# Attention and two feed-forward layers on one core: where the second layer's weights are split and parked

## The chip, the cores and the metric

One core of a Trainium2 chip runs the kernel. Its engines are TensorE (PE in the tables, with PEld for its weight loads), VectorE (DVE), ScalarE (ACT) and GpSimd (POOL); SyncE (SP) issues nearly all DMAs, in order, from one queue. Each engine works through its own list of instructions in order and waits on semaphores. The metric is the device time of one execution in microseconds (us). The kernel before takes 1095.94 us, the median of three runs (1095.74 to 1098.24).

## The reference

`x` is chunked attention over 3072 tokens (8 heads of 64, so 512 columns; each chunk of 32 queries sees 56 keys and 8 memory slots). Two feed-forward layers follow, both 512 to 2048 to 512 columns:

```python
h = x @ w_in                                  # layer 1
x = (h - np.tanh(h)) @ w_out
h = x @ w_in2                                 # layer 2
g = np.maximum(h, 0.0) + alpha * np.minimum(h, 0.0)
out = g @ w_out2
```

The weights come as 64-bit floats. The kernel works in 32 bits and carries each operand as a high part and a low rest, so that a product is three matmuls (high by high, high by rest, rest by high).

## The kernel before, in words

**Layer 1, blocks 0 to 3.** The first 2048 tokens go through attention and layer 1 in four blocks of 512. A block runs over sixteen slices f of 128 hidden columns: 12 matmuls of 128x512 for h (L320), tanh and subtraction (L334, L335), the split of g into `gh` and `gl` (L342, L343), 12 matmuls for y (L361). Attention of the next tokens runs in between: scores into `sp` (L674, in block 0 L716), softmax, values into `pv` (L800). In block 0 all 32 weight words of layer 1 (a word is a 128x512 slice, W_in in tiles `ri`, W_out in `ro`) are loaded and converted from 64 bits, and split into `wt`. Block 0's order is written out by hand; from there on a scheduler places the instructions of each engine.

**The pair and layer 2.** The last 1024 tokens go through layer 1 in another way, and all 3072 tokens through layer 2 in that way too: with seven products of half-size operands in place of eight. There are four such blocks: b = 0 is the pair (layer 1's last 1024 tokens), b = 1 to 3 are layer 2. Each has eight pairs of h slices (`pair_h`, 42 matmuls L455 a pair) and then a y stage (L569). The seven products need sums of weight slices, so the weights are also prepared once in that form and written to DRAM, which the code calls parking: `w1i`, `w1o` for layer 1 and `w2i`, `w2o` for layer 2. The h of block b reads `w1i` or `w2i` by DMA (`wi`, L416), its y `w1o` or `w2o` (`wo`, L407).

**Parking** is a list of steps (`park_plan`). Layer 1's 48 steps take words that are already split. Layer 2's 64 steps load a 64-bit word into `pk` (L105), convert it in two passes on VectorE (L116 `u`, L129 `wv`) and one on ScalarE (L125, from 16 bits to 16 bits, in place), split it (L139, L140), form two or four sums `sm` (L165 to L170 for W_in, L205 to L210 for W_out), split those into `ws`, and store all of it. Four steps make two words into one group: the first word, the second word, the two halves of the sums. W_in and W_out groups alternate. `PARKS` says how many steps go into which block: blocks 0 to 3 and the pair's first four slices. A step's loads are issued ahead of it, its stores right behind it.

**What sets the order.** Raw words and sums live in the pool `w`, which has 35 places; layer 1's weights hold 32 of them until the last block lets them go one by one. In that last block, from f = 2 on, `stage["roomy"]` lets a load go one step earlier. The converted low word `u` lies in the PSUM pool `ps_a`, two banks, which attention's scores `sp` also use. The pair's products 5 and 7 lie in `ps_y` (four banks), in `ps_a` for its first slice.

Of the kernel before, what the change touches and what calls it, by code (L numbers as in the profile page):

```python
# [7 lines left out]
FP32 = mybir.dt.float32  # L8
# [21 lines left out]
PARKS = ((2, 30, 32), (34, 0, 32), (34, 0, 32), (28, 0, 27), (14, 0, 16))  # L30
# [10 lines left out]
def chunk_attention_two_ffn_kernel(  # L41
# [55 lines left out]
    def load_raw(l, i, name):  # L97
# [15 lines left out]
    def shift_word(raw):  # L113
        pool, tag = (ps_y, "y") if stage.get("early") else (ps_a, "a")
        u = pool.tile([128, 512], U32, tag=tag, name="u")
        nc.vector.tensor_scalar(  # L116
            out=u, in0=words_of(raw)[0], scalar1=13, scalar2=None, op0=ALU.logical_shift_right
        )
        return u

    def top_word(raw):
        def part(dtype, k):
            return raw.bitcast(dtype).rearrange("p (n four) -> p n four", four=4)[:, :, k]

        nc.scalar.activation(out=part(FP16, 3), in_=part(BF16, 2), func=ACTF.Copy)  # L125

    def merge_words(raw, u, dst=None):
        s = t_p.tile([128, 512], U32, tag="t", name="s") if dst is None else dst.bitcast(U32)
        nc.vector.scalar_tensor_tensor(  # L129
            out=s, in0=words_of(raw)[1], scalar=0xffff0000, in1=u, op0=ALU.bitwise_and, op1=ALU.bitwise_or  # L130
        )
        return s.bitcast(FP32)

    def to_f32(raw, dst=None):
        top_word(raw)
        return merge_words(raw, shift_word(raw), dst)
# [7 lines left out]
    sw = {}  # L144

    def park_in(f):
        raw = raws.pop((1, 2 * f))
        v = aw.tile([128, 512], FP32, tag="v", name="wv")
# [4 lines left out]
        if odd:  # L153
            split_f32(v[:, 256:512], w[:, 0:256], w[:, 256:512])
            nc.sync.dma_start(out=w2i[p][:, 3072:3584], in_=f32(w)[:, 0:512])
        else:
            split_f32(v, w[:, 0:512], w[:, 512:1024])
            nc.sync.dma_start(out=w2i[p][:, 0:1024], in_=f32(w))

    def park_sum(p, half, to=None):  # L160
# [15 lines left out]
        nc.sync.dma_start(out=(to or w2i)[p][:, c:c + 1024], in_=f32(w))  # L176

    def park_op(m, p, src, to=None):
        c = 512 * (p % 2)
        dst = (to or w2o)[m][p // 2][:, c:c + 512].rearrange("k (a n) -> k a n", a=2)  # L180
        nc.sync.dma_start(out=dst, in_=f32(src))
# [7 lines left out]
    def park_out(f):  # L189
        raw = raws.pop((1, 2 * f + 1))  # L190
        v = aw.tile([128, 512], FP32, tag="v", name="wv")
# [24 lines left out]
    def first_in(p):  # L216
        for odd in range(2):
            w = wts[2 * p + odd, 0]
            v = sw[odd] = aw.tile([128, 512], FP32, tag="v", name="wv")
            add = nc.vector.tensor_tensor if odd else nc.gpsimd.tensor_tensor  # L220
            add(out=v, in0=f32(w[:, 0]), in1=f32(w[:, 1]), op=ALU.add)
            if odd:
                dst = w1i[p][:, 3072:3584].rearrange("p (a n) -> p a n", a=2)
                nc.sync.dma_start(out=dst, in_=f32(w)[:, :, 256:512])
            else:
                nc.sync.dma_start(out=w1i[p][:, 0:1024], in_=f32(w).rearrange("p a n -> p (a n)"))

# [27 lines left out]
    def park_plan():  # L255
        order = [(2 * p + j, side) for p in range(NF // 2) for side in range(2) for j in range(2)]
        loaded = [0]

        def step(fn, *args, n=0):
            def go():  # L260
                n1 = n + (1 if n and stage.get("roomy") else 0)
# [14 lines left out]
        for p in range(NF // 2):  # L276
            for k, (one, total) in enumerate(((park_in, park_sum), (park_out, park_out_sum))):
                n = 4 * p + 2 * k
# [3 lines left out]
                yield step(total, p, 1, n=n + 3)  # L282

# [152 lines left out]
    def split_x2(b, m):  # L436
# [3 lines left out]
        split_f32(f32(src), hi, lo)  # L440
# [33 lines left out]
    def pair_h(i, ahead=None, mid=None):  # L474
# [11 lines left out]
        for m in (1, 6, 5, 7) if p % 2 else (6, 1, 5, 7):  # L486
# [138 lines left out]
    astack = ExitStack()  # L625
# [652 lines left out]
```

## Time and profile before

| what | value |
|---|---|
| time, median of 3 | 1095.94 us |
| profiled execution, its own time | 1097.9 us |
| its span, first to last instruction | 1096.1 us |
| mean granted TensorE clock | 0.982 |
| PE busy | 1045.6 us, 95% of the span |
| DVE, ACT, POOL busy | 768.6, 613.1, 513.0 us |
| DMA | 259.12 MB, mean 236 GB/s |

The stages lie in time like this: attention's start to 28.6 us, block 0 to 137.8, blocks 1, 2 and 3 to about 242.5, 356 and 470.5, the pair's h to about 556, its y to 639, and then layer 2's h and y stages by turns (the first h 639 to 706.5). A stage in which PE is busy to the full gains nothing from other engines' idle time; the time that can be won is where PE is idle or its clock is below full, which is 1.00 in the tables (2.4 GHz; the other level is 1.2 GHz, and a mean between them is a mixture).

### The profile page before, as it was taken

To read this page: it belongs to the slowest core of one execution; us is meant where nothing else is said; L and a number is where in the kernel's file an instruction comes from. 1 tells how busy PE (TensorE), PEld (TensorE's weight loads), DVE (VectorE), ACT (ScalarE), POOL (GpSimd) and SP (SyncE) were. 2 spreads that over 40 slices of the span, in tenths; PEclk is the share of its full clock that TensorE was granted. 3 is DMA by queue.
4 is the path that set the end of the run, shared out by engine and by line. 5 is a ranking of instruction groups with operands and counts; after the bars stand their busy time and mean duration, and the time that the engine had idled before them with its cause. 6 is when DMAs were issued, how large, how long until landed. Compare 5 with 4: busy or idle time off the path is not lost.

```text
span 1096.1 us, 17823 instructions
## 1 busy us (share of the span) xinstructions
PE 1045.6 (95%) x6582; PEld 848.1 (77%) x6582; DVE 768.6 (70%) x1044; ACT 613.1 (56%) x942; POOL 513.0 (47%) x428
## 2 busy tenths in 40 slices
PE   6999999999988799979999999999999999999998
PEld 5777788777766578766778888888788888888886
DVE  6687777778555666668588845689755789656883
ACT  5888654444546676745364446655256844456650
POOL 6576778888655677966221512213322206123100
PEclk8999999999999899989999999999999999999999
DMA  9998545466578888959747867277685289682575
GB/s 327 340 321 277 179 176 212 158 197 219 187 237 264 290 291 296 373 175 410 300 154 247 302 212 249 84 249 235 226 300 199 77 272 306 203 284 87 156 213 168
DMA packets 133095, 259.12 MB, mean 236 GB/s; under 512 B 39056, under 2 KB 73872, under 8 KB 133008
## 3 DMA queue, kind: packets, MB, share of 16 engines
q1 hardware_dynamic: 124368, 251.43, 67.1%
q10 hardware_dynamic: 8640, 6.56, 1.9%
q8 instruction: 52, 0.85, 0.3%
q14 instruction: 35, 0.29, 0.1%
HBM read 184.54 MB, written 73.40 MB: 235 GB/s over the span
## 4 chain that ended last, share of the span: by engine, by line
PE 55%; DVE 3%; DMA 2%; ACT 1%; issue 1%; POOL 0%; SPq 0%; DVEq 0%; ACTq 0%
PE yb L569 27%; PE h L455 25%; PE y L361 1%; PE h L320 1%; DMA wo<-w2o 1%; DMA x<-x0d 1%; DMA pk<-in_moe_w_out_dram 1%; DVE u L116 0%; DMA wi<-w1i 0%; ACT pk L125 0%; DVE wv L129 0%; DVE gb L477 0%; DVE gb L465 0%; DVE xt L431 0%; DVE sm L169 0%
## 5 line engine op out<-in xcount | busy, mean ns | idle before, releaser
L455 PE MATMUL h<-xh,wi 128*128 128x512 f32 x896 | 283.0, 392 | 10.6 <-ACT hv L508 7.1
L569 PE MATMUL yb<-goh,wo 128*128 128x512 f32 x896 | 278.8, 389 | 0.7 <-DMA wo<-w2o 0.7
L455 PEld LDWEIGHTS h<-xh,wi 128*128 128x128 f32 x896 | 169.1, 189 | 50.6 <-ACT hv L508 8.0
L569 PEld LDWEIGHTS yb<-goh,wo 128*128 128x128 f32 x896 | 168.2, 188 | 36.0 <-DMA wo<-w2o 1.1
L320 PE MATMUL h<-ring,wt 128*128 128x512 f32 x768 | 189.3, 395 | 1.1 <-DVE t L335 1.1
L569 PE MATMUL yb<-gol,wo 128*128 128x512 f32 x448 | 174.4, 389 | 0.6 <-DVE gol L542 0.6
L320 PEld LDWEIGHTS h<-ring,wt 128*128 128x128 f32 x768 | 143.8, 189 | 34.5 <-DVE t L335 3.2
L517 POOL TENSOR_TENSOR t<-gb,ga 128x512 f32<-128x512 f32 x32 | 45.2, 1414 | 245.8 <-DVE ga L470 203.7
L361 PE MATMUL y<-gh,wt 128*128 128x512 f32 x512 | 135.9, 405 | 11.3 <-ACT gh L342 8.2
L361 PEld LDWEIGHTS y<-gh,wt 128*128 128x128 f32 x512 | 95.7, 192 | 36.7 <-ACT gh L342 10.2
L455 PE MATMUL h<-xl,wi 128*128 128x512 f32 x256 | 99.9, 390 | 0.0
L569 PEld LDWEIGHTS yb<-gol,wo 128*128 128x128 f32 x448 | 84.1, 188 | 18.4 <-DVE gol L542 1.0
L140 POOL TENSOR_TENSOR ws<-sm,ws 128x512 fp32r<-128x512 f32 x64 | 85.6, 1342 | 20.7 <-ACT ws L139 18.6
L343 POOL TENSOR_TENSOR gl<-t,gh 128x512 fp32r<-128x512 f32 x64 | 87.2, 1363 | 14.6 <-ACT gh L342 7.2
L551 ACT ACTIVATE goh<-ga 128x1024 fp32r<-128x1024 f32 x48 | 48.5, 1051 | 55.2 <-DVE ga L542 47.9
L140 POOL TENSOR_TENSOR x<-x,xh 128x1024 fp32r<-128x1024 f32 x12 | 34.6, 2898 | 94.6 <-ACT xh L139 94.5
L542 DVE TENSOR_TENSOR gol<-ga,goh 128x1024 fp32r<-128x1024 f32 x48 | 65.0, 1381 | 19.0 <-ACT goh L551 19.0
L542 DVE TENSOR_TENSOR gol<-gb,goh 128x1024 fp32r<-128x1024 f32 x48 | 70.2, 1488 | 10.0 <-ACT goh L551 10.0
L551 ACT ACTIVATE goh<-gb 128x1024 fp32r<-128x1024 f32 x48 | 49.6, 1054 | 48.8 <-DVE gb L542 43.9
L455 PE MATMUL h<-x,wi 128*128 128x512 f32 x192 | 75.2, 392 | 0.0
L361 PE MATMUL y<-gl,wt 128*128 128x512 f32 x256 | 70.5, 396 | 0.7 <-POOL gl L343 0.7
L469 ACT ACTIVATE n<-n,alpha_neg 128x512 f32<-128x512 f32 x96 | 64.9, 719 | 0.4
(116 smaller groups left out, 1694.0 us busy)
## 6 DMA issues: line engine op xcount, KB each, us to landing
wo<-w2o SPq DMA_DIRECT2D x84, 512.0 KB, 4.6
wi<-w2i SPq DMA_DIRECT2D x72, 512.0 KB, 5.8
wo<-w1o SPq DMA_DIRECT2D x28, 512.0 KB, 4.5
wi<-w1i SPq DMA_DIRECT2D x24, 512.0 KB, 7.7
kn<-in_k_dram SPq DMA_DIRECT2D x24, 384.0 KB, 5.6
vn<-in_v_dram SPq DMA_DIRECT2D x24, 384.0 KB, 4.2
w1i<-ws SPq DMA_DIRECT2D x16, 512.0 KB, 4.1
w1o<-ws SPq DMA_DIRECT2D x32, 256.0 KB, 2.8
```

What stands on the lines that cost most here:

```text
L140: nc.gpsimd.tensor_tensor(out=lo, in0=v, in1=f32(hi), op=ALU.subtract)
L320: last["ffn"] = nc.tensor.matmul(out=h, lhsT=wi[:, a, kk, :], rhs=ring[c][:, s0:s0 + n, kk, :], start=(i == 0), stop=(i == 3 * KD - 1),).ins
L343: nc.gpsimd.tensor_tensor(out=gl, in0=t, in1=f32(gh), op=ALU.subtract)
L361: mm = nc.tensor.matmul(out=yp[l, b][j][:, :n * 128], lhsT=wo[:, a, j * 128:(j + 1) * 128], rhs=g[c], start=first, stop=final,)
L455: nc.tensor.matmul(out=h, lhsT=w[:, a, 128 * kt:128 * kt + 128], rhs=x[c][:, kt, :], start=(first and j == 0), stop=(j == 5), skip_group_c ...
L469: nc.scalar.activation(out=n, in_=n, func=ACTF.Copy, scale=alpha_neg[:, f:f + 1])
L517: nc.gpsimd.tensor_tensor(out=d3, in0=gb[1], in1=ga[1], op=ALU.subtract)
L542: last["prep"] = nc.vector.tensor_tensor(out=out, in0=p, in1=q, op=op).ins
L551: nc.scalar.activation(out=hi, in_=src, func=ACTF.Copy)
L569: last["yy"] = nc.tensor.matmul(out=yd[b, into][i], lhsT=w[:, a, i], rhs=op[c][:, p % 2], start=(m == into and p == 0 and n == 0), stop=(p ...
```

## The change

- The plan of layer 2's parking first makes all W_in words, then all W_out words. It is thinner in layer 1 (27, 27 and 24 steps in blocks 1 to 3, in place of 34, 34 and 28) and ends earlier in block 3. The W_out words, 32 steps, lie in the pair's h (16 steps over its first six slices) and in layer 2's first h (16 steps over its first four slices).
- A step's stores are kept back and issued at the head of the next step.
- The conversion for parking writes ScalarE's 16-bit result to the destination tile, one of two fixed tiles `wv`, and not into the raw word; VectorE's two passes stay.
- In block 0 the raw words are loaded whole, ScalarE scales the high word into `u` as one 32-bit pass, and VectorE makes three passes of it where there were two.
- Three low parts of the pair's operands are subtracted on VectorE and not on GpSimd. The pair's products 5 and 7 lie in a pool of two banks, opened three slices before layer 1's end. Layer 2's first block loads its first four `wo` from its fifth slice on and not from its second.

```diff
-PARKS = ((2, 30, 32), (34, 0, 32), (34, 0, 32), (28, 0, 27), (14, 0, 16))
+PARKS = ((2, 30, 32), (27, 0, 32), (27, 0, 32), (24, 0, 22), (16, 0, 22), (17, 0, 16))
...
+    def scale_word(raw):
         pool, tag = (ps_y, "y") if stage.get("early") else (ps_a, "a")
         u = pool.tile([128, 512], U32, tag=tag, name="u")
+        nc.scalar.activation(
+            out=u.bitcast(FP32), in_=words_of(raw)[1].bitcast(FP32), func=ACTF.Copy, scale=2.0 ** -112
+        )
+        return u
+
+    def merge_words(raw, u):
+        lw, hw = words_of(raw)
+        nc.vector.tensor_scalar(
+            out=u, in0=u, scalar1=3, scalar2=None, op0=ALU.logical_shift_left
+        )
+        nc.vector.scalar_tensor_tensor(
+            out=u, in0=hw, scalar=0x80000000, in1=u, op0=ALU.bitwise_and, op1=ALU.bitwise_or
+        )
+        s = t_p.tile([128, 512], U32, tag="t", name="s")
+        nc.vector.scalar_tensor_tensor(
+            out=s, in0=lw, scalar=29, in1=u, op0=ALU.logical_shift_right, op1=ALU.bitwise_or
+        )
+        return s.bitcast(FP32)
+
+    def to_f32(raw, dst):
+        top = raw.bitcast(BF16).rearrange("p (n four) -> p n four", four=4)[:, :, 2]
+        out = dst.bitcast(FP16).rearrange("p (n two) -> p n two", two=2)[:, :, 1]
+        nc.scalar.activation(out=out, in_=top, func=ACTF.Copy)
+        pool, tag = stage["u"]
...
+    def store_now():
+        for dst, src in stores:
+            nc.sync.dma_start(out=dst, in_=src)
+        stores.clear()
...
     def park_plan():
-        order = [(2 * p + j, side) for p in range(NF // 2) for side in range(2) for j in range(2)]
+        order = [(f, side) for side in range(2) for f in range(NF)]
         loaded = [0]
 
         def step(fn, *args, n=0):
             def go():
+                store_now()
                 n1 = n + (1 if n and stage.get("roomy") else 0)
...
-        split_f32(f32(src), hi, lo)
+        if b == 0 and m in (6, 7, 4):
+            nc.scalar.activation(out=hi, in_=f32(src), func=ACTF.Copy)
+            nc.vector.tensor_tensor(out=lo, in0=f32(src), in1=f32(hi), op=ALU.subtract)
+        else:
+            split_f32(f32(src), hi, lo)
...
-            elif mid:
-                d[m] = ps_a.tile([128, 512], FP32, tag="a", name="h2")
-            elif b == 0:
-                d[m] = ps_y.tile([128, 512], FP32, tag="y", name="h2")
             else:
                 d[m] = ps_h2.tile([128, 512], FP32, tag="h2", name="h2")
...
+                if b == 1 and p > 3:
+                    load_out(b * NO + p - 4)
+                if b != 1 and 0 < p < 5:
...
-                if b == 0 and p < PAIR_FREE:
+                if b < 2:
                     for x in range(4):
-                        parked_pair(4 * p + x)
+                        parked_pair(b, 4 * p + x)
```

Three places in the order of the instructions are spoken of later.

VectorE in block 0, from one slice's `t` (the subtraction of tanh) to the next, first before, then changed (`ro` and `ri` are raw words of W_out and W_in, `s` the converted word, `et` and `ebuf` attention's):

```order
L335 TENSOR_TENSOR t<-h,t 128x512
L116 TENSOR_SCALAR u<-ro 128x512
L129 SCALAR_TENSOR_TENSOR s<-ro,u 128x512
L768 STREAM_TRANSPOSE et<-sc 128x512
L116 TENSOR_SCALAR u<-ri 128x512
L129 SCALAR_TENSOR_TENSOR s<-ri,u 128x512
L784 COPY ebuf<-et 32x8x32 x2
L335 TENSOR_TENSOR t<-h,t 128x512
```

```order
L362 TENSOR_TENSOR t<-h,t 128x512
L126 TENSOR_SCALAR u<-u 128x512
L129 SCALAR_TENSOR_TENSOR u<-ro,u 128x512
L133 SCALAR_TENSOR_TENSOR s<-ro,u 128x512
L800 STREAM_TRANSPOSE et<-sc 128x512
L126 TENSOR_SCALAR u<-u 128x512
L129 SCALAR_TENSOR_TENSOR u<-ri,u 128x512
L133 SCALAR_TENSOR_TENSOR s<-ri,u 128x512
L816 COPY ebuf<-et 32x8x32 x2
L362 TENSOR_TENSOR t<-h,t 128x512
```

Two passes more stand between one `t` and the next.

SyncE where layer 2's parking begins, in block 2, first before, then changed (`pk` are raw words coming in, `w2i` and `w2o` stores, `kn`, `qn` and `vn` attention's loads):

```order
L158 DMA w2i_90<-pk 128x1024
L155 DMA w2i_90<-pk 128x512
L105 DMA pk<-in_moe_w_out_dram 128x2047
L176 DMA w2i_90<-ws 128x1024 x2
L181 DMA w2o_0_98<-pk 128x2x256
L658 DMA vn<-in_v_dram 96x1024
L105 DMA pk<-in_moe_w_out_dram 128x2047
L105 DMA pk<-in_moe_w_in_dram 128x2047
L181 DMA w2o_0_102<-pk 128x2x256
L181 DMA w2o_0_110<-pk 128x2x256
```

```order
L168 DMA w2i_90<-pk 128x1024
L168 DMA w2i_90<-pk 128x512
L108 DMA pk<-in_moe_w_in_dram 128x2047
L168 DMA w2i_90<-ws 128x1024
L690 DMA vn<-in_v_dram 96x1024
L168 DMA w2i_90<-ws 128x1024
L108 DMA pk<-in_moe_w_in_dram 128x2047
L676 DMA kn<-in_k_dram 128x768
L683 DMA qn<-in_q_dram 128x512
L168 DMA w2i_91<-pk 128x1024
```

Where a W_in group was followed by a W_out group with seven small stores, another W_in group with four stores follows; one of its `ws` stores now stands behind the load of `vn`.

ScalarE in layer 2's first h, from the second slice's `hs` on, first before, then changed (`hs`, `hv`, `n` belong to the slices; `pk`, `wv`, `ws` to parking):

```order
L499 ACTIVATE hs<-h_6924 128x512
L468 ACTIVATE n<-h_6844 128x512
L469 ACTIVATE n<-n,alpha_neg 128x512
L508 ACTIVATE hv<-h_6926 128x512
L468 ACTIVATE n<-gb_6839 128x512
```

```order
L526 ACTIVATE hs<-h_6788 128x512
L499 ACTIVATE n<-h_6673 128x512
L500 ACTIVATE n<-n,alpha_neg 128x512
L154 ACTIVATE ws<-sm 128x512 x2
L141 ACTIVATE wv_160<-pk 128x512
L535 ACTIVATE hv<-h_6790 128x512
L141 ACTIVATE wv_161<-pk 128x512
L154 ACTIVATE pk<-wv_160 128x4x2x32
L499 ACTIVATE n<-gb_6668 128x512
```

Parking's passes stand in the slices' own queue, some of them ahead of `hv`. From the second slice's `hs` to the fifth's the changed order holds six first passes (`wv<-pk`), nine splits of 256 columns (`pk<-wv`) and eight of 512 (`ws<-sm`) that were not there.

## Rows read from the trace of the kernel before

**Rows 1.** the page: busy time by engine, then PE and its clock in 40 slices.

```profile
PE 1045.6 (95%) x6582; PEld 848.1 (77%) x6582; DVE 768.6 (70%) x1044; ACT 613.1 (56%) x942; POOL 513.0 (47%) x428
PE   6999999999988799979999999999999999999998
PEclk8999999999999899989999999999999999999999
```

**Rows 2.** busy us (x instructions) by stretch, then clock, DMA share, GB/s.

```profile
28.60:137.80 109.20, 106.69 (x854) 83.20 (x855) 81.52 (x130) 88.75 (x132) 73.94 (x65) 1.00 0.80 277
242.50:287.90 45.40, 41.24 (x428) 31.82 (x429) 33.14 (x54) 21.59 (x40) 35.59 (x33) 0.96 0.63 204
287.90:380.00 92.10, 76.59 (x651) 60.51 (x650) 53.78 (x100) 54.16 (x88) 53.94 (x58) 0.91 0.76 248
380.00:470.50 90.50, 88.38 (x585) 71.26 (x584) 57.48 (x93) 61.75 (x99) 71.72 (x63) 1.00 0.90 322
470.50:556.00 85.50, 75.51 (x314) 59.13 (x313) 60.97 (x90) 41.05 (x68) 41.51 (x33) 0.96 0.70 267
639.00:706.50 67.50, 67.50 (x299) 55.91 (x298) 37.85 (x57) 42.73 (x73) 18.88 (x14) 1.00 0.60 203
```

**Rows 3.** who PE waited for, 290 to 400: us, times, longest.

```profile
PE sp L674 <- DVE wv L129: 11.5, 3, 6.9
```

**Rows 4.** VectorE's pass u, 300 to 380: busy, mean ns, idle before.

```profile
L116 DVE TENSOR_SCALAR u<-pk 128x512 uint32<-128x512 uint32 x11 | 7.6, 691 | 16.0 <-DMA pk<-in_moe_w_out_dram 12.4 <-DMA pk<-in_moe_w_in_dram 3.6
```

**Rows 5.** timeline: start, us, engine, line, [idle before <- releaser].

```profile
363.01 0.33 SPq L176 DMA_DIRECT2D w2i<-ws  x1
365.65 0.33 SPq L105 DMA_DIRECT2D pk<-in_moe_w_out_dram  x1
370.34 0.69 DVE L116 TENSOR_SCALAR u<-pk 128x512 uint32<-128x512 uint32 x1 [4.31 <-DMA pk<-in_moe_w_out_dram]
371.79 0.69 DVE L129 SCALAR_TENSOR_TENSOR wv<-pk,u 128x512 uint32<-128x512 uint32 x1 [0.76 <-ACT pk L125]
372.53 1.08 PE L674 MATMUL sp<-kn,qn 64*32 64x64 f32 x32 [6.94 <-DVE wv L129]
```

**Rows 6.** busy us in two short stretches, columns as in rows 2.

```profile
480.00:485.00 5.00, 2.29 (x11) 1.56 (x9) 4.76 (x7) 1.43 (x3) 2.88 (x3) 1.00 0.00 0
485.00:490.00 5.00, 1.22 (x3) 1.03 (x4) 4.26 (x8) 3.66 (x7) 3.54 (x4) 0.59 0.62 197
```

**Rows 7.** groups of the whole run: count, busy us, mean ns, idle before.

```profile
L125 ACT ACTIVATE pk<-pk 128x512 f16<-128x512 bf16 x32 | 43.8, 1368 | 21.7 <-DMA pk<-in_moe_w_out_dram 16.0 <-DMA pk<-in_moe_w_in_dram 4.8 <-issue 0.9
L468 ACT ACTIVATE n<-h 128x512 f32<-128x512 f32 x72 | 42.0, 590 | 2.5 <-PE h L455 2.5
L139 ACT ACTIVATE ws<-sm 128x512 fp32r<-128x512 f32 x64 | 40.1, 631 | 41.3 <-DVE sm L166 14.6 <-DVE sm L243 9.1 <-DVE sm L206 4.9
L139 ACT ACTIVATE pk<-wv 128x256 fp32r<-128x256 f32 x32 | 12.5, 413 | 9.5 <-DVE wv L129 9.5
L116 DVE TENSOR_SCALAR u<-pk 128x512 uint32<-128x512 uint32 x32 | 21.8, 687 | 25.1 <-DMA pk<-in_moe_w_out_dram 18.5 <-DMA pk<-in_moe_w_in_dram 6.5
L129 DVE SCALAR_TENSOR_TENSOR wv<-pk,u 128x512 uint32<-128x512 uint32 x32 | 21.8, 683 | 10.8 <-ACT pk L125 10.5
L206 DVE TENSOR_TENSOR sm<-sm,wv 128x256 f32<-128x256 f32 x8 | 7.5, 944 | 0.1
L209 DVE TENSOR_TENSOR sm<-wv 128x256 f32<-128x256 f32 x8 | 5.0, 621 | 0.0
```

**Rows 8.** two slices of the pair's h, three of layer 2's first.

```profile
496.95:520.30 23.35, 20.95 (x88) 15.64 (x86) 20.25 (x34) 14.46 (x25) 15.16 (x13) 1.00 1.04 410
651.20:679.80 28.60, 28.60 (x128) 23.67 (x127) 15.89 (x24) 17.15 (x32) 7.76 (x6) 1.00 0.75 259
```

**Rows 9.** the sum sm of L206, 470 to 556, as in rows 7.

```profile
L206 DVE TENSOR_TENSOR sm<-sm,wv 128x256 f32<-128x256 f32 x2 | 2.5, 1234 | 0.0
```

**Rows 10.** 18.6 us of block 0.

```profile
66.60:85.20 18.60, 18.24 (x165) 14.61 (x164) 15.20 (x26) 17.15 (x26) 13.14 (x13) 1.00 0.90 320
```

More of the change, by code (lines that the diff above doesn't have):

```diff
@@ L104, in load_raw @@
                 after.enter_context(tc.issue_after(last["load"]))
-            last["load"] = nc.sync.dma_start(
-                out=raw.bitcast(U16)[:, 0:2047], in_=src.bitcast(U16)[:, 1:2048]).ins
+            if l == 0:
+                last["load"] = nc.sync.dma_start(out=raw, in_=src).ins
+            else:
+                last["load"] = nc.sync.dma_start(
+                    out=raw.bitcast(U16)[:, 0:2047], in_=src.bitcast(U16)[:, 1:2048]).ins
         raws[l, i] = raw
@@ L118, in shift_word @@
         )
[L119 to L128, printed above, removed]
         nc.vector.scalar_tensor_tensor(
-            out=s, in0=words_of(raw)[1], scalar=0xffff0000, in1=u, op0=ALU.bitwise_and, op1=ALU.bitwise_or
+            out=s, in0=s, scalar=0xffff0000, in1=u, op0=ALU.bitwise_and, op1=ALU.bitwise_or
         )
[L132 to L136, printed above, removed]
+        return dst
     def split_f32(v, hi, lo):
@@ L144, in chunk_attention_two_ffn_kernel, with store @@
     sw = {}
+    stores = []
+    def store(dst, src):
+        stores.append((dst, src))
+    def store_now():
+        for dst, src in stores:
+            nc.sync.dma_start(out=dst, in_=src)
+        stores.clear()
     def park_in(f):
         raw = raws.pop((1, 2 * f))
-        v = aw.tile([128, 512], FP32, tag="v", name="wv")
+        v = wvs[f % 2]
         v = to_f32(raw, v)
@@ L175, in park_sum @@
         c = 1024 * (1 + half)
-        nc.sync.dma_start(out=(to or w2i)[p][:, c:c + 1024], in_=f32(w))
+        store((to or w2i)[p][:, c:c + 1024], f32(w))
     def park_op(m, p, src, to=None):
@@ L180, in park_op @@
         dst = (to or w2o)[m][p // 2][:, c:c + 512].rearrange("k (a n) -> k a n", a=2)
-        nc.sync.dma_start(out=dst, in_=f32(src))
+        store(dst, f32(src))
     def by_tile(x):
@@ L275, in park_plan @@
             yield step(first_out_sum, p, 1, n=1 if p == NF // 2 - 1 else 0)
-        for p in range(NF // 2):
-            for k, (one, total) in enumerate(((park_in, park_sum), (park_out, park_out_sum))):
-                n = 4 * p + 2 * k
+        for side, (one, total) in enumerate(((park_in, park_sum), (park_out, park_out_sum))):
+            for p in range(NF // 2):
+                n = NF * side + 2 * p
                 yield step(one, 2 * p, n=n + 2)
@@ L625, in chunk_attention_two_ffn_kernel @@
     astack = ExitStack()
+    wv_p = ctx.enter_context(tc.tile_pool(name="wv", bufs=1))
+    wvs = [wv_p.tile([128, 512], FP32, name=f"wv{j}") for j in range(2)]
+    for x in wvs:
+        nc.gpsimd.memset(x, 0.0)
     ac = astack.enter_context(tc.tile_pool(name="ac", bufs=1))
@@ L628, in chunk_attention_two_ffn_kernel @@
     ps_a = astack.enter_context(tc.tile_pool(name="ps_a", bufs=2, space=PSUM))
+    stage["u"] = ps_a, "a"
     KW = CH + W + NM
@@ L1147, in parked_pair @@
                 next(park)()
-        def no_more_parking():
-            assert next(park, None) is None
-            astack.close()
-            with tc.issue_after(last["pre"]):
-                nc.vector.tensor_scalar(
-                    out=alpha_neg, in0=alpha_sb, scalar1=-1.0, scalar2=None, op0=ALU.mult
-                )
-            stage["z"] = ctx.enter_context(tc.tile_pool(name="z", bufs=4))
         for b in range(NB):
@@ L1161, in chunk_attention_two_ffn_kernel @@
                 i = b * P2 + p
+                if b < 2 and p == 0:
+                    stage["u"] = (ps_h, "h") if b else (ps_y, "y")
                 if b == 0 and p == PAIR_FREE:
-                    no_more_parking()
-                    ps_h2 = ctx.enter_context(tc.tile_pool(name="ps_h2", bufs=2, space=PSUM))
+                    with tc.issue_after(last["pre"]):
+                        nc.vector.tensor_scalar(
+                            out=alpha_neg, in0=alpha_sb, scalar1=-1.0, scalar2=None, op0=ALU.mult
+                        )
+                if b == 1 and p == PAIR_FREE:
+                    assert next(park, None) is None
                 if p == P2 - 1:
```

36 lines of the change are left out of this document (21 added, 15 removed).

## The prediction, made before the changed kernel was run

> **What bounds the kernel now.** The page comes first: PE is busy 95% of the span, and its slices show where it isn't: the first, and those from about 200 to 375 us and 480 to 520 us, where the clock falls too [rows 1]. From 556 us to the end all but a few slices are full, so nothing can be won there, only lost. The second view is the table by stretch [rows 2]. Of it the reader is to take two columns, PE busy and the clock. What a stretch loses is its idle time plus busy time times (1 - clock), an estimate for what the lower clock costs. Block 0 loses 2.5 us. From block 1's end to layer 2's first parked word (242.5 to 287.9) it is 4.2 + 1.6. The stretch 287.9 to 380 loses 15.5 + 6.9 = 22.4. The rest of block 3 loses 2.1, though its DMA share of 0.90 is higher. The pair's h loses 10.0 + 3.0 = 13.0. Layer 2's first h loses nothing.
>
> The third view is the waits. In 290 to 400 PE stood 11.5 us before attention's scores `sp`, for VectorE's pass `wv` of a parked word [rows 3]: both use the two banks of `ps_a`. That pass in turn waited for its word: `u` sat idle 16.0 us before 11 words, 12.4 of it for W_out words and 3.6 for W_in words [rows 4]. One such stop in full: SyncE issues the store of `ws`, then the load of the second W_out word at 365.65, VectorE's passes start at 370.34 and 371.79, and PE goes on at 372.53 after 6.94 us of idling [rows 5]. After 380, where the pool `w` has more free places, such stops are gone [rows 2]. In the pair's h the worst place is 480 to 490: PE is busy 3.5 of 10 us, at a clock that falls to 0.59, while VectorE is busy 9.0 [rows 6].
>
> **The change, part by part.** The sum is made against the profiled execution, 1097.9 us (its span of 1096.1 and 1.8 around it), which is 2.0 above the median of the runs; the 2.0 is taken off at the end.
>
> *Parking in layer 1.* The stretch that loses 22.4 us holds some 13 words (11 in 80 us [rows 4]), so 26 steps, with few free places in `w`, W_in and W_out groups by turns: 0.86 us a step. In the change 8 steps of layer 2's parking are left in block 2 and about 4 in block 3 before f = 2, all of W_in. At 0.86 a step these 12 cost 10.3, which saves 12.1. If only waits for W_in words count (3.6 of 16.0), they cost less than half of that, and 17 to 18 is saved. The stretch before it (5.8 lost) has no conversions but denser sums; 27 steps for 34 may give 1 to 2 of it. Against that: stores a step later hold a place of `w` longer, and the order shows one `ws` store behind the load of `vn`. If each remaining step cost 1.4 us, the gain would be 5. I take -14, between -5 and -20, nearest to the rate per step. What is late next in these blocks is the chain from h over tanh to `gh`, which I leave at what it loses now.
>
> *The pair's h.* Before, 14 steps lie in four slices and the other four slices are free; now 16 steps lie in six, and the work on VectorE is spread evenly. The two slices 496.95 to 520.3, full of parking, took 23.35 us, against 28.6 / 3 = 9.53 a slice without it: 2.1 us lost a slice with VectorE busy 87% [rows 8]. The first two slices lose the rest, at 480 to 490. In the change six slices carry 2.7 steps each and not 3.5. If the cost falls in proportion, 1.6 a slice is 9.8; if an engine below its limit costs little, 3 remain. With 5 to 6 left the gain is 7. Bounds -11 and -2: products 5 and 7 now have two banks and not four, so PE can run less far ahead.
>
> *Layer 2's first h.* Three of its slices take 28.6 us, PE full, VectorE busy 15.89, ScalarE 17.15, DMA at 259 GB/s [rows 8]. The order puts between the second slice's `hs` and the fifth's three groups of parking. On ScalarE: 6 x 1.368 + 9 x 0.413 + 8 x 0.631 = 17.0, so 34.1 in all [rows 7, 8]. On VectorE: 6 x (0.687 + 0.683) for two passes and 12 sums at 0.78, the mean of the dearest and the cheapest, together 17.6, so 33.5. On the DMA engines: a group loads two words of 0.524 MB and stores seven pieces of 0.262 MB, so 8.6 MB come to 7.4, of which some 1.3 for `wo` (one of 0.524 a slice) move behind; 14.7 MB at 410 GB/s, what the busy stretch reached, are 36 us. All three want 33 to 36 us where PE wants 28.6, so nothing covers this work, and 5 to 7 us are lost at the least over three slices, less a little that later slices absorb. The nearest row with all three engines so loaded is 496.95 to 520.3: 2.1 us a slice. Four slices make 8.6, and ScalarE has two passes for each `n` here where the pair has one: I take +9. Below, +4; above, +20, if two or three slices stop as at 480 to 490.
>
> The first pass is the largest part that ScalarE gets. Its row is 1.368 us for 512 columns, more than twice the 0.590 of `n` with as many [rows 7]. The Trainium skill ("ScalarE: Activation LUTs", What ACT_TABLE_LOAD costs) gives an ACTIVATE one element a cycle whatever its type, 186 ns + 0.833 ns a column, so 0.61 us by it. The row contradicts that for this 16-bit pass. If the new destination brought it to that figure, ScalarE would want 29.6 and not 34.1, but VectorE and DMA would still want 33 to 36.
>
> *Block 0.* 32 words get a third pass: 32 x 0.687 = 22.0 us more on VectorE, less about 2 for an addition and three sums that fall behind the block. VectorE goes from 81.5 to 101.5 of 109.2 us [rows 2, 7]. In a tight 18.6 us, VectorE is busy 15.20 [rows 10]; the share of 32 words in 109.2 us is 5.5 words, whose third passes make it 19.0, so for four such stretches it is just past full, and `t`, for which `gh` and then PE wait, stands behind them in the queue. Excess 0.4 x 4 gives 1.6, at 95% use 5. ScalarE loses some 25 us of work by the shorter pass, but beside it PE is busy 18.24 of the 18.6 us as it is. I take +2, between 0 and +6.
>
> *At nothing.* Whole raw loads in block 0: ScalarE's passes of it never waited for a word. The low parts moved to VectorE lie at block 3's end, where PE loses little. The later `wo` loads have three slices, some 28 us, before the first y needs them.
>
> Sum: -14 - 7 + 9 + 2 = -10, so 1087.9, and 1086 us against the median.
>
> **The rivals.**
>
> *Slower: layer 2's first h gets into the state of 480 to 490.* Here each `hv` and `n` stands behind parked passes that wait for a word, so one late load stops ScalarE, VectorE and PE together, and the clock falls as it did there to 0.59. That place lost 6.5 us of idling and some more by the clock, about 8; three of them are 24. With the other terms the sum is +5: 1101 us. It ends slower once that h lasts 86.5 us and not 67.5. For it: the three totals above 33 us, and 410 GB/s wanted. Against it: the pair's later slices, as full, lost 2.1 each.
>
> *No difference: free places in `w` are the limit.* Then the longer hold of deferred stores eats what the fewer steps save: -4 in place of -14, so the sum is 0 and the time 1096. For it: the load at 365.65 went out only after a store [rows 5]. Against it: the W_out words, seven stores each group, had most of the waits.
>
> *No difference: VectorE and GpSimd disturb each other.* The sum of L206 takes 0.944 us on the average and 1.234 in the pair's h, beside GpSimd's splits [rows 7, 9]. At 1.23 for every sum VectorE would want 33.5 + 12 x 0.45 = 38.9 us in the three slices, 10 over PE; with four slices and some of it in the pair's h too, +9 becomes +17, and the time 1094. The Trainium skill ("GPSIMD Engine Reference", Specifications) says that GpSimd shares its SBUF interfaces with VectorE and collides with instructions with two SBUF inputs, which these sums are; the two rows agree in direction.
>
> *Faster still: the spread parking hides.* -19 in layer 1, -9 in the pair, +5 in layer 2: with block 0 at +2 the sum is -21: 1075 us. For it: W_in words hardly waited [rows 4].
>
> **How the numbers follow.** My forecast (1079 to 1092) gets 0.50, faster still 0.14, the two with no difference 0.08 each, slower 0.20. Differences under 0.3%, about 3.3 us (1092.6 to 1099.2), are what a measurement of this kernel can't tell from none. So faster is 0.50 + 0.14 + a part of the 1094 case (0.02) = 0.66, the same 0.14, slower 0.20. The range leaves 0.1 out at each end: 1073 to 1102, the terms' own bounds (-27 and +19 about 1096) not all meeting at once. The forecast's own range is 1079 to 1092.
>
> **What would show it.** In the profile after: PE's wait of `sp` for the last pass of a parked word in blocks 2 and 3 falls from 11.5 us to under 5, and the clock there is 0.95 or better in every slice of the page. The pair's h takes about 78 us with no stretch like 480 to 490. Layer 2's first h takes about 76 us, ScalarE and VectorE over 85% busy in its first four slices, PE waiting for `hv` or `n`; the later h stages stay at 67. Block 0 lasts 111, with PE waiting for `gh`. I am wrong if layer 1's blocks still stop for parked words, or if layer 2's first h loses over 20 us.

## The result, and the profile after

| | before | after |
|---|---|---|
| time, median of 3 | 1095.94 us | 1080.49 us (1079.83 to 1081.48) |
| ratio | | 0.9854, 95% interval 0.983 to 0.9877 |
| span of the profiled execution | 1096.1 us | 1078.7 us |
| mean granted clock | 0.982 | 0.989 |

The prediction was 1086 us, faster. The page of after, to be read against [rows 1]: busy time, PE by slices, its clock.

```profile
PE 1042.7 (97%) x6582; PEld 847.0 (79%) x6582; DVE 790.4 (73%) x1079; ACT 581.8 (54%) x942; POOL 509.4 (47%) x427
PE   7999999999998999998999988999999999999998
PEclk9999999999998999999999999999999999999999
```

For the sum both executions are cut at the same events: PE's first matmul of block 0, the first `ys` copy on VectorE of blocks 0 and 1, the last of layer 1, and ScalarE's `hs` of the eighth slice in the pair's h and in layer 2's first h. The columns are those of [rows 2]; the stretches are the start, block 0, block 1, blocks 2 and 3 in two parts, the pair's h, the pair's y with layer 2's first h, the rest. First before:

```profile
0.00:29.21 29.21, 20.20 (x439) 18.15 (x439) 18.17 (x40) 16.74 (x34) 16.60 (x26) 0.82 0.95 332
29.21:137.82 108.61, 106.09 (x850) 82.61 (x849) 81.52 (x130) 88.19 (x131) 73.94 (x65) 1.00 0.80 276
137.82:243.27 105.45, 102.89 (x969) 83.04 (x967) 79.95 (x135) 50.14 (x96) 86.08 (x83) 1.00 0.53 186
243.27:364.75 121.48, 109.52 (x992) 85.70 (x992) 76.84 (x136) 67.04 (x114) 80.91 (x82) 0.96 0.69 227
364.75:470.70 105.95, 96.88 (x678) 78.05 (x675) 67.04 (x110) 69.91 (x111) 79.89 (x71) 0.95 0.91 318
470.70:545.70 75.00, 65.57 (x272) 51.22 (x271) 54.86 (x82) 35.62 (x61) 38.73 (x31) 0.95 0.80 304
545.70:698.77 153.07, 152.51 (x673) 125.98 (x672) 106.41 (x115) 79.88 (x115) 42.18 (x23) 1.00 0.63 220
```

Then after:

```profile
0.00:27.86 27.86, 19.80 (x438) 17.49 (x439) 18.97 (x41) 16.00 (x34) 17.54 (x28) 0.94 0.94 323
27.86:133.49 105.63, 104.78 (x844) 81.47 (x844) 91.71 (x159) 71.14 (x130) 72.07 (x64) 1.00 0.85 288
133.49:234.55 101.06, 100.77 (x965) 82.50 (x964) 68.89 (x126) 48.46 (x90) 77.47 (x77) 1.00 0.50 175
234.55:338.57 104.02, 102.32 (x971) 83.27 (x969) 70.79 (x121) 52.46 (x97) 74.93 (x75) 1.00 0.59 193
338.57:447.00 108.43, 101.69 (x711) 82.44 (x712) 73.02 (x105) 59.41 (x103) 72.25 (x61) 0.95 0.79 282
447.00:520.54 73.54, 67.85 (x276) 52.85 (x275) 58.38 (x88) 38.55 (x70) 37.50 (x34) 0.95 0.94 339
520.54:682.36 161.82, 154.20 (x660) 123.52 (x659) 124.83 (x143) 90.38 (x137) 62.93 (x42) 0.99 0.78 273
```

The difference, stretch by stretch: start -1.4, block 0 -3.0, block 1 -4.4, blocks 2 and 3 -15.0 (227.4 to 212.4), the pair's h -1.5, its y and layer 2's first h +8.8, the rest -1.0: together the -17.4 of the spans. PE's 11.5 us before `sp` for a parked word [rows 3] are gone; the longest wait for `sp` that is left in 290 to 400 us is for attention's own pass:

```profile
PE sp L706 <- DVE sc L732: 2.8, 1, 2.8
```

The pair's h still stops. Ten us of it, and below them the stop in order of time (columns as in [rows 5], other lines left out):

```profile
500.00:510.00 10.00, 7.11 (x29) 5.29 (x28) 8.50 (x13) 5.87 (x11) 5.61 (x6) 0.94 0.77 290
```

```profile
504.31 1.29 POOL L545 TENSOR_TENSOR ga<-ga,ga 128x512 f32<-128x512 f32 x1
504.67 1.21 DVE L230 TENSOR_TENSOR sm<-wv,wv 128x256 f32<-128x256 f32 x1
505.56 1.78 POOL L155 TENSOR_TENSOR pk<-wv,pk 128x256 fp32r<-128x256 f32 x2
505.81 0.95 DVE L234 TENSOR_TENSOR sm<-wv 128x256 f32<-128x256 f32 x1
506.69 0.94 DVE L231 TENSOR_TENSOR sm<-sm,wv 128x256 f32<-128x256 f32 x1
507.66 0.63 ACT L154 ACTIVATE ws<-sm 128x512 fp32r<-128x512 f32 x1 [2.22 <-DVE sm L231]
507.66 0.42 DVE L235 TENSOR_TENSOR sm<-wv,sm 128x256 f32<-128x256 f32 x1
508.20 0.76 ACT L141 ACTIVATE wv<-pk 128x512 f16<-128x512 bf16 x1
508.83 0.57 ACT L526 ACTIVATE hs<-h 128x512 f32<-128x512 f32 x1
509.45 0.79 PE L486 MATMUL h<-xh,wi 128*128 128x512 f32 x1 [2.79 <-ACT hs L526]
```

The slice's `hs` stands on ScalarE behind a parked split, which waits for VectorE's sums; PE waits for `hs`. Of the 5.7 us that PE idles in the pair's h, 4.0 are waits for `hs` and 1.1 for `hv`. Three of the sums last 1.21, 0.95 and 0.94 us beside GpSimd's passes, and the fourth 0.42 behind them; by an estimate from these rows 1.8 of the 2.22 us for which ScalarE stood are that meeting. Layer 2's first h is slowed as well: 620 to 660 us has PE busy 33.6 of 40.

```profile
620.00:640.00 20.00, 16.97 (x70) 12.56 (x70) 17.53 (x30) 16.23 (x31) 10.76 (x10) 1.00 0.99 333
640.00:660.00 20.00, 16.60 (x67) 12.25 (x66) 14.63 (x24) 12.43 (x23) 14.35 (x13) 0.97 1.04 381
```

### The profile page after: what moved, and what is told of

It is laid out like the page before. It is cut to its first block, busy times and chain, and to the rows that moved or that the text cites. A ratio compares the mean times of both kernels' runs of the same rounds, so it can differ in the third digit from the quotient of the medians.

```text
span 1078.7 us, 17896 instructions
## 1 busy us (share of the span) xinstructions
PE 1042.7 (97%) x6582; PEld 847.0 (79%) x6582; DVE 790.4 (73%) x1079; ACT 581.8 (54%) x942; POOL 509.4 (47%) x427
## 4 chain that ended last, share of the span: by engine, by line
PE 51%; DVE 6%; ACT 2%; issue 1%; POOL 1%; DMA 0%; DVEq 0%; ACTq 0%; POOLq 0%
PE yb L596 27%; PE h L486 23%; PE y L388 1%; DVE gb L569 1%; DVE sm L231 1%; ACT n L499 0%; DMA w2o<-ws 0%; DVE gb L508 0%; DVE ga L496 0%; DVE gol L569 0%; ACT n L500 0%; DVE h L508 0%; DVE xl L469 0%; DVE gb L496 0%; DVE sm L230 0%
## 5 line engine op out<-in xcount | busy, mean ns | idle before, releaser
L486 PE MATMUL h<-xh,wi 128*128 128x512 f32 x896 | 288.7, 397 | 13.3 <-ACT hs L526 7.2
L544 POOL TENSOR_TENSOR t<-gb,ga 128x512 f32<-128x512 f32 x32 | 45.7, 1429 | 207.9 <-DVE ga L501 172.4
L388 PE MATMUL y<-gh,wt 128*128 128x512 f32 x512 | 133.7, 402 | 4.6 <-ACT gh L369 4.6
L155 POOL TENSOR_TENSOR x<-x,xh 128x1024 fp32r<-128x1024 f32 x12 | 38.1, 3190 | 96.5 <-ACT xh L154 96.5
L362 DVE TENSOR_TENSOR t<-h,t 128x512 f32<-128x512 f32 x64 | 43.7, 683 | 33.3 <-ACT t L361 33.1
```

What stands on the lines that cost most here:

```text
L155: nc.gpsimd.tensor_tensor(out=lo, in0=v, in1=f32(hi), op=ALU.subtract)
L362: last["dve"] = nc.vector.tensor_tensor(out=t, in0=h, in1=t, op=ALU.subtract).ins
L388: mm = nc.tensor.matmul(out=yp[l, b][j][:, :n * 128], lhsT=wo[:, a, j * 128:(j + 1) * 128], rhs=g[c], start=first, stop=final,)
L486: nc.tensor.matmul(out=h, lhsT=w[:, a, 128 * kt:128 * kt + 128], rhs=x[c][:, kt, :], start=(first and j == 0), stop=(j == 5), skip_group_c ...
L544: nc.gpsimd.tensor_tensor(out=d3, in0=gb[1], in1=ga[1], op=ALU.subtract)
```

## The experiments

They ran in three sets, on three chips, each set with its own runs of the kernel before. In the last set the changed kernel itself ran once more, and it came out at 0.9794 of before, where it had been 0.9854: so kernels of different sets are told apart by their times only when they differ by more than some 0.6%, and below that by the stretches of their traces. After and x13_again are one kernel, and their stretches differ by 2.6 us in blocks 2 and 3, 0.8 in the pair and 1.3 in L2; smaller differences than these say nothing. All stretches in one table, cut as above (us, one profiled execution each; "pair" is the pair's h, "L2" the pair's y with layer 2's first h):

| kernel | ratio to before, interval | block 0 | block 1 | blocks 2, 3 | pair | L2 |
|---|---|---|---|---|---|---|
| before | 1 | 108.6 | 105.5 | 227.4 | 75.0 | 153.1 |
| after | 0.9854, 0.983 to 0.9877 | 105.6 | 101.1 | 212.4 | 73.5 | 161.8 |
| x13_again | 0.9794, 0.9772 to 0.9817 | 105.6 | 101.1 | 209.8 | 72.7 | 163.1 |
| x1_conv | 1.0101, 1.008 to 1.0122 | 106.4 | 105.3 | 244.1 | 75.9 | 153.1 |
| x2_stores | 0.9816, 0.9785 to 0.9848 | 105.7 | 101.1 | 207.9 | 72.6 | 160.9 |
| x3_turns | 0.9832, 0.9807 to 0.9857 | 105.7 | 101.1 | 214.4 | 70.7 | 159.9 |
| x4_spread | 0.9798, 0.9777 to 0.9819 | 105.7 | 101.1 | 215.0 | 72.3 | 158.3 |
| x5_inplace | 0.9894, 0.9879 to 0.9909 | 105.8 | 101.1 | 211.5 | 72.4 | 166.6 |
| x6_dense | 1.0, 0.9985 to 1.0016 | 106.6 | 105.7 | 229.9 | 74.7 | 155.0 |
| x8_old0 | 0.9817, 0.979 to 0.9844 | 105.9 | 101.1 | 208.5 | 70.9 | 161.2 |
| x9_even | 0.9751, 0.9717 to 0.9785 | 105.7 | 101.5 | 210.0 | 66.3 | 157.6 |
| x10_late | 0.9749, 0.9726 to 0.9772 | 105.7 | 101.1 | 206.5 | 73.2 | 158.7 |
| x11_even0 | 0.9726, 0.9706 to 0.9747 | 106.0 | 101.1 | 212.3 | 66.3 | 157.6 |
| x12_only | 0.9814, 0.9793 to 0.9834 | 105.9 | 101.1 | 219.8 | 66.0 | 156.8 |

**Dense parking with all the rest of the change (x6_dense).**

```diff
-PARKS = ((2, 30, 32), (27, 0, 32), (27, 0, 32), (24, 0, 22), (16, 0, 22), (17, 0, 16))
+PARKS = ((2, 30, 32), (34, 0, 32), (34, 0, 32), (28, 0, 27), (15, 0, 16), (0, 0, 16))
```

> The changed kernel with parking as dense as before: 34 steps in blocks 1 and 2, 28 in block 3, 15 in the pair's h, none in layer 2's first h; W_in words first, stores a step later, block 0 as changed. Theory A (thinning is what layer 1 gained): from block 1's end to layer 1's last ys it takes 225 to 245 us again and not 208 to 215, layer 2's first h loses nothing, and the time is 1088 us (1084 to 1098). Theory B (order of the words, the new buffers and the deferred stores are what layer 1 gained): that stretch stays at 212 to 217 us, the h of layer 2 gives back its 9, and the time is 1073 us (1070 to 1077).

It took 1096.65 us beside 1096.57 of before. The whole gain goes, and every stretch behind block 0 is within 2.5 us of before: A. The stop of [rows 5] is back, and this time for a W_in word, since no W_out word comes so early. PE's waits in blocks 1 to 3 and one of them in time:

```profile
PE sp L706 <- DVE wv L148: 8.6, 3, 6.7
```

```profile
359.58 0.33 SPq L108 DMA_DIRECT2D pk<-in_moe_w_in_dram  x1
365.61 0.69 DVE L145 TENSOR_SCALAR u<-pk 128x512 uint32<-128x512 uint32 x1 [4.92 <-DMA pk<-in_moe_w_in_dram]
366.42 0.69 DVE L148 SCALAR_TENSOR_TENSOR wv<-wv,u 128x512 uint32<-128x512 uint32 x1
367.16 1.08 PE L706 MATMUL sp<-kn,qn 64*32 64x64 f32 x32 [6.69 <-DVE wv L148]
```

The load goes out 6.0 us before its word is there, VectorE has come to that word's pass already, and PE stands 6.69 us, as it did before for a W_out word. So the number of steps in a block brings the stop back. Why a load is late at that number, by the order in SyncE's queue, by free places of `w` or by the chain of the step ahead of it, no run separates.

**Groups by turns again (x3_turns).**

```diff
-        order = [(f, side) for side in range(2) for f in range(NF)]
+        order = [(2 * p + j, side) for p in range(NF // 2) for side in range(2) for j in range(2)]
```

(and the plan's two loops exchanged in the same way).

> The changed kernel with W_in and W_out groups by turns as before, the same number of steps in every part. Theory A (the prediction's: the W_out words, with seven small stores a group, had most of the waits in layer 1): blocks 2 and 3 lose about 5 us again, 1085 us (1083 to 1089), with PE waiting for a parked word there. Theory B (fewer steps in layer 1 is the whole gain): 1080 us (1079 to 1082) whatever the order. Since W_out words then come earlier and W_in words fall into layer 2's first h, that h may move by a few us as well; it is read apart.

It took 1078.44 us: B. With thin parking PE waits for no parked word in blocks 2 and 3, W_out words or not; these blocks took 214.4 us, among the 207.9 to 215.0 of the other versions with 27, 27 and 24 steps and the short first pass. Which kind of word came first made no difference that shows.

**Stores at once (x2_stores).**

```diff
-        stores.append((dst, src))
+        nc.sync.dma_start(out=dst, in_=src)
```

> The changed kernel with each store of parking issued in its own step and not in the next. Theory A (the deferral is part of what took layer 1's stops away: a store in SyncE's queue stands before its split has run, and the raw loads behind it come late): PE's waits in blocks 2 and 3 and in the pair's h rise again, 1085 us (1083 to 1089). Theory B (it only holds places of w longer, as the prediction had it): the same or a little faster, 1080 us (1077 to 1081.5).

It took 1077.33 us, blocks 2 and 3 were the shortest of all with 27, 27 and 24 steps, and the h stages didn't grow: B. In thin parking the deferral is worth nothing that can be told.

**Block 0's conversion alone, and all but it (x1_conv, x8_old0).** The first is the kernel before with block 0's whole loads and three VectorE passes, the second the changed kernel with the old two passes there:

```diff
-            half_w[i] = half_w[i], scale_word(half_w[i])
+            top_word(half_w[i])
...
-            half_w[i] = merge_words(*half_w[i])
+            half_w[i] = merge2(half_w[i], shift_word(half_w[i]))
```

> The kernel before with only the first block's conversion changed (whole raw words loaded, ScalarE's scaling pass, three VectorE passes); parking is as before. Theory A (ScalarE's shorter pass and fewer meetings with GpSimd on VectorE outweigh the third pass): the block ends about 4 us earlier, 1092 us (1090 to 1094), and VectorE's busy time between the first h and the block's end is about 91 us, not 101. Theory B (the prediction's: VectorE past full delays t): the block ends 2 us later, 1098 us. If the time stays at 1096, the block's gain in the changed kernel comes from another part of the change.

> The changed kernel with block 0's conversion as before (shifted raw loads, ScalarE's 16-bit pass in place, two VectorE passes); the rest as changed. Theory A (block 0's own gain of about 4 us, and nothing of it elsewhere): block 0 ends at about 137.5 us, layer 1 after it takes as long as in the changed kernel, 1084 us (1082 to 1087). Theory B (what happens in block 0 shifts the parking behind it, as in the kernel before with block 0 changed, where blocks 2 and 3 took 17 us more): the time differs from that by 5 us or more either way.

x1_conv took 1108.59 us, which neither theory gave. Its block 0 ended 4.0 us earlier, as A had it (2.2 us shorter, and begun earlier), with VectorE busy 93.8 us of it, but blocks 2 and 3 went from 227.4 to 244.1 us. Parking there is as dense as before, though on ScalarE and VectorE it also stands in another order among the slices' instructions, since the scheduler placed it anew. PE's waits in blocks 2 and 3 have the stop known by now, longer, and 12.4 us for `gh` where it was 5.4:

```profile
PE sp L699 <- DVE wv L132: 13.8, 2, 12.3
```

x8_old0 has the old conversion and yet a block 0 of 105.9 us, 0.3 more than after; it took 1075.18 us. So the conversion is worth nothing within a few tenths of a us, and dense parking is what a small shift can throw about by 17 us. Neither of x8's theories gave its time: A's 1084 us supposed that block 0's conversion was worth 4, and B's shift of the parking didn't come, since blocks 2 and 3 took 208.5 us, no longer than the changed kernel's 209.8 and 212.4. Block 0 of before is 2.7 us longer than x8_old0's, with the same conversion: 1.4 us of it are idling, mostly one wait of y for `gh` at 36.7 us that x8_old0 doesn't have, and 1.2 more matmul time in the stretch. Where that wait comes from stays open. The traced execution began at a granted clock of 0.82, but x2_stores and x5_inplace began at such clocks too and took 105.7 and 105.8.

**The first pass in place (x5_inplace).**

```diff
-        out = dst.bitcast(FP16).rearrange("p (n two) -> p n two", two=2)[:, :, 1]
+        out = raw.bitcast(FP16).rearrange("p (n four) -> p n four", four=4)[:, :, 3]
...
-            out=s, in0=s, scalar=0xffff0000, in1=u, op0=ALU.bitwise_and, op1=ALU.bitwise_or
+            out=s, in0=words_of(raw)[1], scalar=0xffff0000, in1=u, op0=ALU.bitwise_and, op1=ALU.bitwise_or
```

> The changed kernel with ScalarE's first pass of a parked word written in place in the raw word, as before, and not into the new buffer. Its duration should go back from 0.784 to about 1.37 us for each of the 32 words, 18.7 us more on ScalarE. Theory A (ScalarE's queue sets the loss in the h stages with parking): most of the words lie in the pair's h and layer 2's first h, these lose 4 to 8 us more, 1085 us (1083 to 1089). Theory B (VectorE, the transfers and the chain of each group set it): 1080 us (1077 to 1082).

It took 1084.84 us; its ratio is above both of after's, by 0.4% over the first, so the stretches decide. The pass, first here and then in after:

```profile
L141 ACT ACTIVATE pk<-pk 128x512 f16<-128x512 bf16 x32 | 43.7, 1367 | 13.4 <-DMA pk<-in_moe_w_in_dram 13.4
```

```profile
L141 ACT ACTIVATE wv<-pk 128x512 f16<-128x512 bf16 x32 | 25.0, 784 | 14.3 <-DMA pk<-in_moe_w_in_dram 13.8 <-DVE sm L234 0.4
```

L2 takes 166.6 us for 161.8 and 163.1, the other stretches are as they were: 3.5 to 4.8 us, A in kind and at its lower end. Some 2 us at the most of that are idling of PE (9.4 us for 7.6 and 8.7), the rest is PE at a lower clock (0.97 for 0.99). Six of the 32 words get this pass in L2 and eight in the pair's h, which didn't grow. So the short pass saves about 4 us where the parking is densest. Its edit changes the destination and with it where VectorE's second pass reads; that pass takes 684 ns here and 682 in after.

**The same steps over more slices (x4_spread, x9_even).** x4_spread changes the last entry alone (17, 0, 26); x9_even changes both h stages, as below, and issues each store in its own step:

```diff
-PARKS = ((2, 30, 32), (27, 0, 32), (27, 0, 32), (24, 0, 22), (16, 0, 22), (17, 0, 16))
+PARKS = ((2, 30, 32), (27, 0, 32), (27, 0, 32), (24, 0, 22), (16, 0, 28), (17, 0, 28))
```

> The changed kernel with the 17 steps of layer 2's first h spread over 26 positions (six and a half slices) and not 16 (four slices). Theory A (the prediction's: three engines and the DMA want 33 to 36 us where PE wants 28.6, so it is density that costs): the h's loss of 11 us falls to 3 to 5, 1074 us (1072 to 1077). Theory B (each group stops PE once for its chain of word, passes, sum and split, however far apart the groups are): the loss stays, 1080 us (1079 to 1082). In between would say that both have a part.

> The changed kernel with the 16 steps of the pair's h and the 17 of layer 2's first h spread evenly over 28 positions each (seven slices), and stores issued at once. Theory A (density costs): the pair's h, slice 1 to slice 8, takes 74 to 78 us and not 80.8, layer 2's first h loses 3 to 6 us and not 9, and the time is 1071 us (1068 to 1074). Theory B (each group costs its stop wherever it lies, and the last slices only get what the earlier ones lose): as with the spread in layer 2 alone, 1074 us (1073 to 1078).

x4_spread took 1074.44 us, by its time not to be told from x13_again; L2 fell from 161.8 and 163.1 to 158.3, so what L2 takes more than before went from 8.8 and 10.1 to 5.2, just short of A's 3 to 5, with A's time. x9_even took 1068.25 us: A, with L2 4.5 us over before, and the pair's h from slice 1 to slice 8 at 73.5 us, a little under A's 74 to 78. The pair's h and L2 of it:

```profile
445.03:511.33 66.30, 64.41 (x271) 49.75 (x271) 53.85 (x84) 33.99 (x64) 32.56 (x31) 1.00 0.95 346
511.33:668.96 157.63, 153.54 (x663) 123.04 (x662) 122.01 (x144) 92.55 (x141) 61.67 (x43) 1.00 0.80 286
```

With the same 16 steps, PE idles 1.9 us in the pair's h and not 5.7, at a clock of 1.00 and not 0.95, although VectorE is busy 81% of it and was 79% in after, ScalarE 51% and 52%, the DMA engines 95% and 94%: it isn't an engine's total that makes the stops. Nor is it the meeting with GpSimd alone, since the pair's sixteen sums last 0.90 us each on the average here and 0.94 in after.

**How steep it is (x10_late).**

```diff
-PARKS = (..., (24, 0, 22), (16, 0, 28), (17, 0, 28))
+PARKS = (..., (18, 4, 22), (19, 0, 28), (20, 0, 28))
```

> The evenly spread version with six steps less in block 3 (18 over positions 4 to 22, none in its first four), three more in each of the two h stages (19 and 20 over 28 positions). Theory A (block 3's start, 335 to 360 us, where PE is busy 18.3 of 24.5 us, stops for a parked word's load ahead of attention's passes on VectorE): block 3 gains 3 to 5, the two h stages lose 1 to 2 together, 1066 us (1063 to 1068). Theory B (that stop is attention's own, and the h stages lose in proportion or more): 1069 us (1068 to 1073).

It took 1071.76 us, no better: B's time, with A's part for block 3. The edit above is against x9_even. Blocks 2 and 3 gained 3.5 and 5.8 us on x9_even and x11_even0, as A had it, but three steps more in the pair's seven slices cost 6.9 us, more than in proportion:

```profile
441.50:514.73 73.23, 67.33 (x280) 52.78 (x279) 59.59 (x91) 37.31 (x69) 36.88 (x33) 0.98 0.86 314
```

At 16 / 7 = 2.3 steps a slice the pair's h takes 66.3 us, at 19 / 7 = 2.7 it takes 73.2, at 16 / 5.5 = 2.9 it takes 70.7 to 73.5, at 14 / 4 = 3.5 (before, in four slices, the others free) 75.0. Part of this spread is the clock, between 0.95 and 1.00 from one execution to the next; PE's idle time alone is 1.9 us at 2.3 steps, 5.9 at 2.7, 5.1 to 6.6 at 2.9 and 9.4 before. So the cost drops between 2.7 and 2.3 steps, and 2.7 can't be told from 2.9. The pair's h of x10_late also has W_in words in it, where x9_even has W_out words alone; but so has x12_only (below), whose pair's h takes 66.0 us.

**The best version, and how much the other parts are worth (x11_even0, x12_only, x13_again).** x11_even0 is x9_even with block 0's old conversion. x12_only also has the groups by turns and the first pass in place, so that of the whole change little but the places of parking is left.

> The kernel with both h stages spread evenly over seven slices and stores at once, and block 0's conversion in two passes as before the change. Theory A (the three-pass conversion is worth nothing within 2 us, since block 0 took 105.6 us from its first h with it and 105.9 with the old one): 1068 us (1066 to 1070.5). Theory B (VectorE's third passes cost, as the prediction had it): 1064 us (1062 to 1066).

> Only the places of parking: evenly spread over seven slices of both h stages and thinner in layer 1, but W_in and W_out by turns, stores at once, the first pass in place in the raw word and block 0's conversion in two passes, all as in the kernel before. Theory A (where the steps lie is all but the whole gain; the in-place pass costs some 4 us where ScalarE stands between slices, as in the changed kernel): 1071 us (1068 to 1075). Theory B (the other parts together hold a third of the gain or more): 1080 us or above.

> The changed kernel itself once more, beside the others of this call, to see how far its own executions lie apart. Theory A (what one execution does at the start and in block 3 makes a few us): executions from 1075 to 1083 us, median 1079 (1077 to 1082). Theory B (it is as narrow as its three executions so far): 1079.8 to 1081.5.

x11_even0 took 1068.6 us: A, the three passes are worth nothing, though VectorE is busy 79.0 us in block 0 with two and 91.7 (after) with three. It beats both kernels; against the changed one it is 0.7% faster in the same set. x9_even beats before by its time, and the changed kernel by its stretches. x12_only took 1077.8 us, between the theories: spreading alone gives two thirds of the best version's gain (1.9 of 2.7%). Its h stages are as short as those of x11_even0; the 7.5 us more lie in blocks 2 and 3 (219.8 and 212.3). In-place pass and turns were put back together, so which of them costs there is open; with turns alone (x3_turns) it was 214.4. x13_again: B fell, and A holds in kind alone, since its median of 1075.91 us lies below A's 1077 to 1082. Over both sets the changed kernel's executions lie between 1074.81 and 1081.48, wider than its first three showed.

## Why the prediction was right, and where it wasn't

- **Parking in layer 1** (-14, between -5 and -20, and 1 to 2 in the stretch before): blocks 2 and 3, which hold both, gave 15.0. The size held. Block 1, which the sum left out, gave 4.4 more: 2.3 are idling (2.6 us before, 0.3 after), and 2.1 are five matmuls of block 2's h that ran inside the stretch before and behind it after, so this part is only moved. One reason given was wrong: that W_out words with their seven stores made the waits, read from 12.4 of 16.0 us of idle time [rows 4]. x6_dense stopped as long for W_in words, and x3_turns didn't stop for W_out words. The row told which word came next, not why it was late; with the steps of a block thinned the stops went, and with them dense they came back (x6_dense).
- **The pair's h** (-7, between -11 and -2): this is the step that failed. By the cut it gave 1.5 us (2.3 in x13_again); by what the stretch loses (idle time plus busy time times 1 - clock) it went from 12.7 to 9.1, so -3.6, and some 2 us of PE's work moved into it. "With 5 to 6 left" was a choice between 9.8 (in proportion to the steps) and 3; 9.1 were left, and 6.7 in x13_again. The two ends went by the number of steps and by how full VectorE is, and the cost follows neither: 2.7 steps a slice lose 7.2 us (x10_late), 2.3 lose 1.9 (x9_even), with VectorE busy 81% in both. What stops PE in the rows above is an order in a queue (`hs` behind a split that waits for sums), not a total; no run moved `hs` ahead of the split, so this is read from the traces and not tested by itself.
- **Layer 2's first h** (+9, between +4 and +20): +8.8, and +10.1 in x13_again. The size held. Its working took the first pass at 1.368 us, but the new destination made it 0.784, and the text said that this wouldn't matter, VectorE and DMA still wanting 33 to 36 us; x5_inplace shows 3.5 to 4.8 us. So two errors offset each other, which is luck: with the old pass the term would have been +13.5. The 0.61 us that the Trainium skill's formula gave ("ScalarE: Activation LUTs", What ACT_TABLE_LOAD costs) is reached by neither destination. VectorE and ScalarE were not over 85% busy in the first four slices, as forecast, but 80% and 72% of 620 to 660 us: the slices stopped instead of filling up.
- **Block 0** (+2, between 0 and +6): -3.0, and -1.4 in the start. The sign was wrong, and the working too: VectorE reached 91.7 us and not 101.5, and PE waited 0.4 us for `gh`. Of the missing 10 us 6.6 are small operations on VectorE that got shorter (below), and 2.5 come from the addition and the sums that fell behind the block, 4.5 us and not 2; so the stretch was never past full. By x8_old0 and x11_even0 the conversion is worth 0.4 us at the most.
- **The rivals.** Layer 2's first h did not fall into the state of 480 to 490 us: in its emptiest 10 us (648 to 658) PE is busy 6.60 at a clock of 1.00. Free places in `w` did not eat the gain, and in thin parking the deferral, held or not, moved nothing; whether they are what makes dense parking late was not tested. VectorE and GpSimd did disturb each other: the sums of L231 took 1.163 us on the average where L206, the same sums before, took 0.944 [rows 7]. The price is inside the +8.8, and how much of it that is no run shows.
- **The sum** was -10 and became -17.4: 6.4 of the difference from block 0 and the start, 4.4 from block 1, 1.0 from blocks 2 and 3, 1.0 from the rest, 0.2 from layer 2's first h, and 5.5 the other way from the pair's h. That the time came out inside 1079 to 1092 is in part luck: the pair and block 0 lie outside their own bounds, on opposite sides, and in the third set the same kernel took 1075.91 us, below that range.

## What to carry to other kernels

Background work that shares in-order queues with a pipeline is priced by how many of its steps stand between two links of the pipeline, and not by the engines' totals alone: put it thinly everywhere that has room, stages whose matmul engine is full included, and look for the count a slice at which the stops end. An idle row that names the transfer says which one came next, not that this kind is slow; move the kinds about before believing it. Run the base kernel again in each set before small differences are read.

## What the hardware showed beside this

ScalarE's 16-bit to 16-bit pass of 512 columns takes 1.367 us written in place in the 64-bit words and 0.784 written to a tile of 32-bit words; the 32-bit pass of block 0 (L119, of after) takes 0.63.

A VectorE instruction that meets a GpSimd addition can last as long as that addition. Block 0 of x8_old0, then of after, in time:

```profile
51.95 1.29 POOL L173 TENSOR_TENSOR wt<-s,wt 128x512 fp32r<-128x512 f32 x1
52.16 1.11 DVE L804 TENSOR_SCALAR sg<-sg 128x8 f32<-128x8 f32 x1
```

```profile
52.21 1.30 POOL L155 TENSOR_TENSOR wt<-s,wt 128x512 fp32r<-128x512 f32 x1
53.58 0.17 DVE L786 TENSOR_SCALAR sg<-sg 128x8 f32<-128x8 f32 x1
54.13 1.05 POOL L792 TENSOR_TENSOR sc<-sc,sg 128x512 f32<-128x512 f32 x1 [0.63 <-ACT wt L154]
```

Eight columns took 1.11 us beside the addition, the two ending at 53.27 and 53.24 us, and 0.17 us in GpSimd's gap. In block 0 ten copies of 32x256 took 0.677 us each in the one and 0.390 in the other. The longer conversion moved these instructions off GpSimd's additions. That is the main reason why third passes of some 22 us made VectorE only 10 us busier than before. The Trainium skill ("GPSIMD Engine Reference", Specifications) names two kinds of VectorE instructions that collide with GpSimd, those with two SBUF inputs and those in a two-port mode. The first kind is the sums of the prediction; the instruction above has one input, and which mode it ran in no run here shows.
